# Top-k attention with a gated feed-forward: the left-over queries of each two batches moved next to each other, scores one slot sooner, another order of the first loads

## The chip, the cores and the metric

The kernel runs on one core of one Trainium2 chip. Time is the device time of one execution in microseconds (us). Before the change it is 1578.04 us, the median of 9 runs (1575.66 to 1578.78).

The engines are named as in the profile: PE (matrix multiply; PEld is its weight load), DVE (vector), ACT (scalar and activation), POOL (GpSimd), SP (issues the DMAs). Each takes its instructions strictly in the order of the program and waits for the others by semaphores.

## The reference

Queries, keys and values are (8 batches, 8 heads, 576 positions, 64 wide), float32. In each row of 576 scores only the 32 largest stay; a softmax of these weights the values. The result, 4608 rows of 512, goes through a feed-forward layer.

```python
scores = scale * np.matmul(q, k.transpose(0, 1, 3, 2))
kth = np.partition(scores, -top_k, axis=-1)[..., -top_k:-top_k + 1]
scores = np.where(scores >= kth, scores, -1000000000.0)
attn = np.exp(scores - np.max(scores, axis=-1, keepdims=True))
attn = attn / (np.sum(attn, axis=-1, keepdims=True) + 1e-09)
x = np.matmul(attn, v)                 # then heads side by side: (4608, 512)
h = x @ w_in                           # 512 x 2048
g = h * np.clip(h + 3.0, 0.0, 6.0) / 6.0
out = g @ w_out                        # 2048 x 512
```

The feed-forward weights arrive as float64 and are converted to float32 bit by bit in the kernel.

## The kernel before

**Tiles.** Two heads make a Pair, two Pairs a Duo. 576 queries are four tiles of 128 and a left-over of 64. A full Duo is one tile of 128 queries for four heads: four rows of 576 scores on each partition (two halves u = 0 and 1, each two rows). A left-over Duo (`self.rest`) holds the 64 left-over queries of four heads, two heads on the lower and two on the upper partitions: one row for each half. Each batch has 8 full and 2 left-over Duos, 80 in all. The list `duos` sets their order.

**Slots.** A Duo is 8 slots. In each slot DVE does one of the four rounds of `top` for one half: MAX8 (L256) finds the 8 largest, MATCH_REPLACE8 (L260) takes them out. All other work is written into slots by hand. For Duo m, at slot 8m plus a number from the table `usual` or `behind`: the shift on POOL (L269, L272), the two exponentials on ACT (L279, L284) and the sum den (L289), its reciprocal on DVE (L293), the scaling on POOL (L303) and the split of the float32 words into 16 bit halves (L312), a DMA transpose issued by SP (flip, L318), the join of the halves (L324, on ACT for u = 0 and on POOL for u = 1, result eT), the weighted values on PE (pv, L344), and their copy into xT or xr on ACT (`place`, L354). The first half's exponentials stand at slot 4, its reciprocal at 9; the second half's at 8 and 13; values at 22, or 25 in most of the run; place one slot later. The last two Duos use a shorter table, `soon`.

`duos[m + 1].scores()` stands in slot 1 of Duo m: matmuls into the PSUM tile big (L222 and L225 for a left-over Duo, L232 and L238 for a full one), then copies into sc by ACT (L227, L228, or L239, L242). In a slot, scores come before the parts of that slot.

**Feed-forward.** When the second half of the heads of a query tile is placed, `queue` adds a block for its 128 rows: 8 pieces of 16 matmuls h (L371) and 8 pieces of 2 matmuls acc (L391). After every second h piece ACT makes g and hs (L379, L381), and POOL gates them two pieces later (L385, L386). The left-over queries of an even batch and of the odd one behind it share the 128 columns of xr, so their block is queued when the odd batch's left-over is placed. Each slot emits about one piece, half a piece in a left-over Duo, one eighth more where 24 or more pieces are left.

**Loads.** In the second half of a batch the Pairs of the next one are loaded by SP, turned by PE (L177) and copied by ACT (L179 to L183). The values of a batch replace those of the batch before (L163, L167); their loads stand in slot 3 of its second and third Duo. Landed data, transposed queries and keys, e16, t16, eT and the raw weights st share the 14 buffers of one pool.

**Weights.** In the first four Duos each slot also moves the conversion of a weight chunk on (32 chunks): ACT makes a and y (L108, L111), POOL bounds a (L109), DVE shifts and merges (L117, L118), POOL adds (L123). a and y live in the 8 buffers of the pool that also holds g.

The order of left-over Duos before: in batches 0 to 2 both behind the last full tile, in 3 to 6 one behind tile 0 and one behind tile 2, in 7 both behind tile 0.

Of the kernel before, what the change touches and what calls it, by code (L numbers as in the profile page):

```python
# [29 lines left out]
def kernel(  # L30
# [9 lines left out]
    nc = tc.nc  # L40
# [47 lines left out]
    def big():  # L88

        return ps_big.tile([P, 5 * 512], F32, tag="big", name="big")  # L90
# [5 lines left out]
    def convert(dst, src):  # L96

        st = kqpool.tile([P, 2 * WC], U32, tag="kq", name="st")
        nc.sync.dma_start(st[:], src)
        yield
        words = st[:].rearrange("p (n two) -> p n two", two=2)
        lo, hi = words[:, :, 0], words[:, :, 1]
        a = gpool.tile([P, WC], F32, tag="g", name="a")
        y = gpool.tile([P, WC], F32, tag="g", name="y")
        nc.scalar.activation(a[:], hi.bitcast(F32), AF.Abs)  # L108
        nc.gpsimd.tensor_scalar(a[:], a[:], HI_MOST, HI_LEAST, ALU.min, ALU.max)  # L109

        nc.scalar.activation(y[:], lo, AF.Copy, bias=2.0, scale=2.0**-51)  # L111
        yield

        au, yu = a[:].bitcast(U32), y[:].bitcast(U32)
        nc.vector.tensor_scalar(au, au, 3, None, ALU.logical_shift_left)  # L117
        nc.vector.scalar_tensor_tensor(  # L118
            out=yu, in0=hi, scalar=0x80000000, in1=yu,
            op0=ALU.bitwise_and, op1=ALU.bitwise_or,  # L120
        )
        yield
        nc.gpsimd.tensor_tensor(  # L123
            dst.bitcast(I32), a[:].bitcast(I32), y[:].bitcast(I32), ALU.add
        )

    def weight_chunks():
# [11 lines left out]
    class Pair:  # L139
# [3 lines left out]
            self.b, self.hp = b, hp  # L143
            self.vm, self.vr, self.kr = vms[hp], vrs[hp], krs[b % 2 * NHP + hp]

        def load(self):
            h0 = 2 * self.hp
            t = self.landed = kqpool.tile([P, 2 * J + 1, 2, D], F32, tag="kq", name="landed")
            for i, src in enumerate((k, q)):
                for hh in range(2):  # L150
                    nc.sync.dma_start(  # L151
                        t[:, i * J : (i + 1) * J, hh, :],
                        src[self.b, h0 + hh, 0:JP, :].rearrange("(p j) d -> p j d", j=J),
                    )
                nc.sync.dma_start(
                    t[i * R : (i + 1) * R, 2 * J, :, :],
                    src[self.b, h0 : h0 + 2, JP:S, :].rearrange("h s d -> s h d"),
                )
# [9 lines left out]
                    self.vr[hh * R : (hh + 1) * R, hh, :], v[self.b, h0 + hh, JP:S, :]  # L168
                )

        def transpose(self):
            kq = kqpool.tile([P, JP + S], F32, tag="kq", name="kq")
            self.kT, self.qT = kq[:, 0:JP], kq[:, JP : JP + S]
            ps = big()
            for j in range(2 * J + 1):
                rows = self.landed[:, j, :, :].rearrange("p h d -> p (h d)")
                nc.tensor.transpose(ps[:, j * P : (j + 1) * P], rows, ident[:])  # L177
            c0 = 2 * JP
            nc.scalar.copy(kq[:, 0:c0], ps[:, 0:c0])  # L179
            nc.scalar.copy(kq[:, c0 : c0 + R], ps[:, c0 + R : c0 + 2 * R])  # L180
            for hh in range(2):
                d = slice(hh * D, (hh + 1) * D)
                nc.scalar.copy(self.kr[d, hh, :], ps[d, c0 : c0 + R])  # L183

    class Duo:

# [14 lines left out]
        def scores(self, us=(0, 1)):  # L201

            if us[0] == 0:
                self.sc = scpool.tile([P, 2, 2 * (S + R)], F32, tag="sc", name="sc")
                self.den = mpool.tile([P, 2, 2], F32, tag="den", name="den")
            sc, nu = self.sc[:, us[0] : us[-1] + 1, :], len(us)
            ps = big()
            heads = [slice(0, D), slice(D, P)]
            qs = slice(self.qt * P, min(self.qt * P + P, S))
            banks = ps[:, 0 : 4 * 512].rearrange("p (n s) -> p n s", s=512)  # L210
            left = ps[:, 4 * 512 :]
            if self.rest:


                quarters = [
                    (i, hh, d, heads[u ^ hh])
                    for i, u in enumerate(us)
                    for hh, d in enumerate(heads)
                ]
                for i, hh, d, to in quarters:  # L220
                    pr = self.pairs[us[i]]
                    nc.tensor.matmul(banks[to, i, :], pr.qT[d, qs], pr.kT[d, :])  # L222
                for i, hh, d, to in quarters:
                    pr = self.pairs[us[i]]
                    nc.tensor.matmul(banks[to, 2 + i, 0:R], pr.qT[d, qs], pr.kr[d, hh, :])  # L225
                nc.gpsimd.memset(sc[:, :, S : S + R], 0.0)
                nc.scalar.copy(sc[:, :, 0:JP], banks[:, 0:nu, :])  # L227
                nc.scalar.copy(sc[:, :, JP:S], banks[:, 2 : 2 + nu, 0:R])  # L228
                return
            for i, u in enumerate(us):  # L230
                pr = self.pairs[u]
                nc.tensor.matmul(  # L232
                    left[:, i * P : (i + 1) * P], pr.qT[:, qs], pr.kr[:].rearrange("p h r -> p (h r)")
                )
            for i, u in enumerate(us):
                pr = self.pairs[u]
                for hh, d in enumerate(heads):
                    nc.tensor.matmul(banks[:, 2 * i + hh, :], pr.qT[d, qs], pr.kT[d, :])  # L238
            nc.scalar.copy(  # L239
                sc.rearrange("p u (h s) -> p (u h) s", h=2)[:, :, 0:JP], banks[:, 0 : 2 * nu, :]  # L240
            )
            nc.scalar.copy(  # L242
                sc[:, :, JP : JP + P], left[:, 0 : nu * P].rearrange("p (u r) -> p u r", r=P)
            )

        def row(self, u, t):
            return self.sc[:, u, t * S : (t + 1) * S]
# [162 lines left out]
    duos = []  # L410
    for b in range(B):
        halves = [pairs[b][0:2], pairs[b][2:4]]
        for qt in range(J):
            duos += [Duo(h, qt) for h in halves]


            if qt == (0 if b == B - 1 else J - 1) and not 2 < b < B - 1:
                duos += [Duo(h, J) for h in halves]
            elif 2 < b < B - 1 and qt % 2 == 0:
                duos.append(Duo(halves[qt // 2], J))  # L420
    assert J == NHP == 4
    per_batch = 2 * J + 2
    ND = len(duos)
# [68 lines left out]
    def land(count=1):  # L492

        for _ in range(min(count, len(chunks))):
            c = convert(*chunks.pop(0))
            next(c)
            landing.append(c)

    def convert_step():


        for c in adding:
            next(c, None)
        adding.clear()
        if len(converting) >= 2 or not landing:
            for c in converting[:1]:
                next(c)
            adding.extend(converting[:1])
            del converting[:1]
        if landing:  # L510
            c = landing.pop(0)
            next(c)
            converting.append(c)
        land()
# [4 lines left out]
        return pairs[b + 1][at - first] if b + 1 < B and 0 <= at - first < NHP else None  # L519

    first = pairs[0]
    first[0].load()
    land(2)
    first[1].load()
    first[0].transpose()
    convert_step()
    duos[0].scores((0,))
    convert_step()
    first[2].load()
    convert_step()  # L530
    first[1].transpose()
    duos[0].scores((1,))
    land()

# [5 lines left out]
        shift1=7, exp1=8, inverse1=13, weights1=14, flip1=16, join1=19, values=22, place=23,  # L540
    )

    behind = dict(usual, values=25, place=26)
    early = dict(
        shift0=3, exp0=3, inverse0=4, weights0=4, flip0=5, join0=8,
        shift1=7, exp1=7, inverse1=8, weights1=8, flip1=9, join1=12, values=12, place=13,
# [29 lines left out]
    for m in range(ND + 3):  # L576
        u = duos[m] if m < ND else None
        for i in range(8):
            if u:
                u.top(i // 4, i % 4)  # L580
            if m < 4:
                parts(8 * m + i, False)
            convert_step()
            if m == 0 and i == 0:
                first[3].load()
            if m == 0 and i in (1, 2):
                first[i + 1].transpose()
            if i == (4 if m == 0 else 1) and m + 1 < ND:
                duos[m + 1].scores()
            if m < 4:  # L590
                parts(8 * m + i, True)
            else:
                parts(8 * m + i)
            if m == 0 and i in (1, 4):
                for p in duos[i // 4].pairs:
                    p.load_values()
            if i == 0:
                p = pair_at(m, 4)
                if p:
                    p.load()  # L600
            if i == 3 and u and u.pairs[0].b and 1 <= m % per_batch <= 2:
                for p in duos[m - 1].pairs:
                    p.load_values()
            if i == 5:
                p = pair_at(m, 5)
                if p:
                    p.transpose()

            due += ((left > 0) + (left >= 24) / 8 + (left >= 48) / 8) / (2 if u and u.rest else 1)
            piece(int(due))  # L610
            due -= int(due)
# [36 lines left out]
```

## Time and profile before

| what | value |
|---|---|
| median of 9 runs | 1578.04 us |
| profiled execution, its own time | 1578.04 us |
| its span, first to last instruction | 1576.3 us |
| DVE busy | 1466.7 us (93%) |
| PE busy, PEld busy | 1444.8 us (92%), 1033.7 us (66%) |
| POOL, ACT busy | 1143.1 us (73%), 1097.3 us (70%) |
| mean granted PE clock | 0.961 of full speed |
| DVE MAX8 (L256), all forms | 1152 of about 0.75 us |
| DVE MATCH_REPLACE8 (L260) | 864 of about 0.74 us |

Busy time is the time in which an engine has an instruction under way; matmuls overlap in their pipeline, so a busy PE need not be at its peak. The trace counts a float32 matmul as two instructions, the built order as one. In a timeline line the first number is the start and the second the time taken, both in us, with neighbouring instructions of one kind merged and their number behind an x.

### The profile page before, as it was taken

The numbers are of one execution on the slowest core, as the hardware profiler recorded it, in microseconds if no ns is written. First come the engines' busy times: TensorE is split into PE (matmuls) and PEld (weight loads), VectorE is DVE, ScalarE is ACT, GpSimd is POOL, SyncE is SP. The second block draws the span as 40 slices with busy tenths as digits, with TensorE's granted clock in tenths as the row PEclk, the third lists the DMA queues.
The fourth block names the chain that finished last, engine by engine and source line by source line (L and its number), as shares of the span: only waits on it lengthen the run. The fifth ranks groups of instructions, "written<-read, shape, count | busy, mean of one in ns | idle before, by whom it ended". The sixth has DMA issues, their size and how long they took to land.

```text
span 1576.3 us, 28787 instructions
## 1 busy us (share of the span) xinstructions
PE 1444.8 (92%) x10272; PEld 1033.7 (66%) x10272; DVE 1466.7 (93%) x3105; ACT 1097.3 (70%) x1865; POOL 1143.1 (73%) x1264
## 2 busy tenths in 40 slices
PE   5356799879999999998999999998999999999899
PEld 3142666567767767776777777766777777776675
DVE  6999999999999999999999999999999999999700
ACT  6675776777877777777776786777776786777521
POOL 4868687777867777867687777867687777867831
PEclk9577899989999999999999999999999999999999
DMA  8552544444444543545254544445254443533410
GB/s 237 156 185 42 116 83 79 92 94 99 73 94 86 101 85 78 98 88 116 54 105 81 98 88 83 94 91 113 58 104 81 98 88 82 103 58 68 83 22 14
DMA packets 450319, 144.49 MB, mean 92 GB/s; under 512 B 433280, under 2 KB 441472, under 8 KB 450176
## 3 DMA queue, kind: packets, MB, share of 16 engines
q1 hardware_dynamic: 450176, 142.65, 43.9%
q8 instruction: 81, 1.33, 0.3%
q14 instruction: 62, 0.51, 0.1%
HBM read 45.09 MB, written 9.44 MB: 35 GB/s over the span
## 4 chain that ended last, share of the span: by engine, by line
DVE 75%; PE 14%; issue 4%; POOL 3%; ACT 2%; SPq 1%; DMA 0%; POOLq 0%
DVE m L256 39%; DVE wk L260 34%; PE acc L391 6%; PE h L371 6%; PE pv L344 2%; DVE y L118 1%; DVE a L117 1%; PE big L238 1%; POOL eT L324 1%; POOL e L312 1%; DVE den L293 1%; POOL sc L303 1%; SPq L151 1%; POOL g L386 0%; ACT sc L284 0%
## 5 line engine op out<-in xcount | busy, mean ns | idle before, releaser
L256 DVE MAX8 m<-wk 128x8 f32<-128x576 f32 x864 | 614.3, 749 | 2.2
L391 PE MATMUL acc<-w_out,g 128*128 128x512 f32 x1152 | 519.8, 602 | 16.4 <-POOL g L386 16.4
L371 PE MATMUL h<-xT,w_in 128*128 128x128 f32 x4096 | 484.4, 279 | 18.4 <-ACT xT L354 18.4
L371 PEld LDWEIGHTS h<-xT,w_in 128*128 128x128 f32 x4096 | 473.9, 195 | 40.6 <-ACT xT L354 18.4
L260 DVE MATCH_REPLACE8 wk<-m,wk 128x576 f32<-128x576 f32 x576 | 424.5, 745 | 0.0
L303 POOL TENSOR_SCALAR sc<-sc,den 128x576 f32<-128x576 f32 x288 | 213.2, 750 | 241.0 <-DVE den L293 222.2
L391 PEld LDWEIGHTS acc<-w_out,g 128*128 128x128 f32 x1152 | 214.1, 192 | 264.9 <-issue 239.7
L312 POOL COPY e<-sc 128x2304 uint16<-128x2304 uint16 (+1 forms) x192 | 320.0, 1677 | 10.1
L279 ACT ACTIVATE sc<-sc,m 128x576 f32<-128x576 f32 x288 | 209.8, 774 | 74.1 <-DVE m L256 73.8
L284 ACT ACTIVATE sc<-sc,shift 128x576 f32<-128x576 f32 x288 | 220.2, 768 | 51.8 <-POOL shift L272 49.7
L324 ACT COPY eT<-t 128x2304 uint16<-128x2304 uint16 (+1 forms) x82 | 215.9, 2633 | 45.2 <-DMA t<-e 40.4
L344 PE MATMUL pv<-eT,vm 128*64 128x128 f32 (+1 forms) x2560 | 163.9, 273 | 57.5 <-ACT eT L324 44.1
L260 DVE MATCH_REPLACE8 wk<-m,sc 128x576 f32<-128x576 f32 x288 | 212.2, 744 | 0.0
L324 POOL COPY eT<-t 128x2304 uint16<-128x2304 uint16 (+1 forms) x78 | 203.6, 2611 | 4.5 <-DMA t<-e 4.3
L344 PEld LDWEIGHTS pv<-eT,vm 128*64 128x64 f32 x2560 | 135.0, 141 | 108.7 <-ACT eT L324 49.0
L256 DVE MAX8 m<-sc 128x8 f32<-128x576 f32 x288 | 203.7, 745 | 1.7 <-ACT sc L242 1.7
L386 POOL TENSOR_TENSOR g<-g,hs 128x512 f32<-128x512 f32 x144 | 184.7, 1283 | 12.1
L379 ACT ACTIVATE g<-h,three 128x512 f32<-128x512 f32 x144 | 98.4, 683 | 135.4 <-PE h L371 124.7
L238 PE MATMUL big<-kq 64*128 64x512 f32 x512 | 136.0, 651 | 0.0
L239 ACT COPY sc<-big 128x2048 f32<-128x2048 f32 (+1 forms) x65 | 119.2, 1833 | 18.1 <-PE big L238 17.9
L385 POOL TENSOR_SCALAR g<-g 128x512 f32<-128x512 f32 x144 | 89.0, 618 | 51.9 <-ACT g L379 40.7
L381 ACT COPY hs<-h 128x512 f32<-128x512 f32 x144 | 83.4, 579 | 0.0
(47 smaller groups left out, 1027.7 us busy)
## 6 DMA issues: line engine op xcount, KB each, us to landing
landed<-in_k_dram SPq DMA_DIRECT2D x64, 128.0 KB, 3.1
landed<-in_q_dram SPq DMA_DIRECT2D x64, 128.0 KB, 3.0
st<-in_moe_w_in_dram SPq DMA_DIRECT2D x16, 512.0 KB, 5.2
vm<-in_v_dram SPq DMA_DIRECT2D x64, 128.0 KB, 2.4
st<-in_moe_w_out_dram SPq DMA_DIRECT2D x16, 512.0 KB, 6.3
out_dram<-o SPq DMA_DIRECT2D x32, 256.0 KB, 2.4
t<-e SPq DMA_TRANSPOSE x160, 4.6
landed<-in_k_dram SPq DMA_DIRECT2D x32, 32.0 KB, 2.7
```

What stands on the lines that cost most here:

```text
L238: nc.tensor.matmul(banks[:, 2 * i + hh, :], pr.qT[d, qs], pr.kT[d, :])
L256: nc.vector.max(self.m[u][:, t, 8 * r : 8 * r + 8], self.cur[t])
L260: nc.vector.match_replace(wk, self.m[u][:, t, 8 * r : 8 * r + 8], self.cur[t], LOWEST)
L279: nc.scalar.activation(row, row, AF.Prelu, bias=m[:, t, TOP_K - 1 : TOP_K], scale=-1.0, alpha=FLAT)
L284: nc.scalar.activation(row, row, AF.Exp, bias=self.less[u][:, t : t + 1], scale=-scale / FLAT, accum_out=self.den[:, u, t : t + 1],)
L303: nc.gpsimd.tensor_scalar(row, row, self.den[:, u, t : t + 1], 1.0, ALU.mult, ALU.mult)
L312: nc.gpsimd.tensor_copy(halves[:, :, to : to + c1 - c0], words)
L324: copy(eT[:, 0 : self.nb, :] .rearrange("p c q -> p (c q)") .bitcast(U16) .rearrange("p (x h) -> p h x", h=2), self.t16[u][:, 0 : 2 * self ...
L344: nc.tensor.matmul(pv[hh * D : (hh + 1) * D, u * w : (u + 1) * w], pr.vm[:, hh, c, :] if c < J else pr.vr[:, hh, :], rhs, start=(c == 0), ...
L371: nc.tensor.matmul(h[:, (f - f0) * P : (f - f0 + 1) * P], w_in[:, i, f * P : (f + 1) * P], xT[:, i, :], start=(i == 0), stop=(i == NHP - 1),)
L386: nc.gpsimd.tensor_tensor(g[:], g[:], hs[:], ALU.mult)
L391: nc.tensor.matmul(acc[:], gs[f // nf][:, f % nf * P : (f % nf + 1) * P], w_out[:, f, :], start=(f == 0), stop=(f == NFC - 1),)
```

## The change

1. **Order of the Duos.** The left-over Duos of an even batch come last in it, those of an odd batch first: four left-over Duos stand in a row at the border of batches 0 and 1, 2 and 3, 4 and 5, 6 and 7.
2. **Scores** of the next Duo stand in slot 0 instead of 1 (Duo 0 keeps its own place), so before the second exponentials of the Duo before, which stand in slot 0 too. In the table `behind` values move from 25 to 24, place from 26 to 25.
3. **The first batch.** The q of the first Pair is loaded from ACT's queue, while k is loaded from SP's; one weight chunk is loaded behind each of the second and third Pair instead of two behind the first; the fourth Pair is loaded before the loop instead of in its first slot. The first Pair is turned through three small PSUM tiles with smaller copies, of which two wait until the first scores are copied. The first half's scores are copied in three pieces, the left-over columns first. Ahead of it all DVE fills a slice of w_out with zeros and PE does two matmuls on it.
4. **Conversion.** y has no buffer of its own any more; it is made in place in the converted weights.

```diff
-        y = gpool.tile([P, WC], F32, tag="g", name="y")
...
-        nc.scalar.activation(y[:], lo, AF.Copy, bias=2.0, scale=2.0**-51)
+        nc.scalar.activation(dst, lo, AF.Copy, bias=2.0, scale=2.0**-51)
...
-        def load(self):
+        def load(self, queue=None):
...
-            for i, src in enumerate((k, q)):
+            for i, (src, eng) in enumerate(((k, nc.sync), (q, queue or nc.sync))):
...
+            if first:
+                ps = [ps_w.tile([P, 512], F32, tag="w", name="kqp") for _ in range(3)]
+                turn(ps[0], range(J))
+                turn(ps[1], [J, 2 * J])
+                turn(ps[2], range(J + 1, 2 * J))
+                nc.scalar.copy(self.kT, ps[0][:])
+                nc.scalar.copy(kq[:, JP : JP + P], ps[1][:, 0:P])
+                copy_left(ps[1][:, P:])
+                self.later = [
+                    (kq[:, JP + P : c0], ps[2][:, 0 : JP - P]),
+                    (kq[:, c0 : c0 + R], ps[1][:, P + R : 2 * P]),
+                ]
+                return
...
+            if us == (0,):
+                (to, src), rest = copies
+                copies = [rest, (to[:, 0, :], src[:, 0, :]), (to[:, 1, :], src[:, 1, :])]
...
-        for qt in range(J):
+        for qt in [J, *range(J)] if b % 2 else range(J + 1):
             duos += [Duo(h, qt) for h in halves]
-            if qt == (0 if b == B - 1 else J - 1) and not 2 < b < B - 1:
-                duos += [Duo(h, J) for h in halves]
-            elif 2 < b < B - 1 and qt % 2 == 0:
-                duos.append(Duo(halves[qt // 2], J))
...
-    first[0].load()
-    land(2)
+    nc.vector.memset(w_out[:, 0, :], 0.0)
+    ps = big()
+    for _ in range(2):
+        nc.tensor.matmul(ps[:, 0:DM], w_out[:, 0, 0:P], w_out[:, 0, :])
+    first[0].load(nc.scalar)
     first[1].load()
-    first[0].transpose()
+    land()
+    first[2].load()
+    land()
+    first[0].transpose(first=True)
+    duos[0].scores((0,))
+    for copy in first[0].later:
+        nc.scalar.copy(*copy)
     convert_step()
-    duos[0].scores((0,))
+    first[3].load()
+    first[1].transpose()
     convert_step()
-    first[2].load()
-    convert_step()
-    first[1].transpose()
     duos[0].scores((1,))
...
-    behind = dict(usual, values=25, place=26)
+    behind = dict(usual, values=24, place=25)
...
-            if m == 0 and i == 0:
-                first[3].load()
...
-            if i == (4 if m == 0 else 1) and m + 1 < ND:
+            if i == (4 if m == 0 else 0) and m + 1 < ND:
                 duos[m + 1].scores()
```

More of the change, by code (lines that the diff above doesn't have):

```diff
@@ L106, in convert @@
         a = gpool.tile([P, WC], F32, tag="g", name="a")
-        y = gpool.tile([P, WC], F32, tag="g", name="y")
         nc.scalar.activation(a[:], hi.bitcast(F32), AF.Abs)
         nc.gpsimd.tensor_scalar(a[:], a[:], HI_MOST, HI_LEAST, ALU.min, ALU.max)
-        nc.scalar.activation(y[:], lo, AF.Copy, bias=2.0, scale=2.0**-51)
+        nc.scalar.activation(dst, lo, AF.Copy, bias=2.0, scale=2.0**-51)
         yield
-        au, yu = a[:].bitcast(U32), y[:].bitcast(U32)
+        au = a[:].bitcast(U32)
         nc.vector.tensor_scalar(au, au, 3, None, ALU.logical_shift_left)
         nc.vector.scalar_tensor_tensor(
-            out=yu, in0=hi, scalar=0x80000000, in1=yu,
+            out=dst.bitcast(U32), in0=hi, scalar=0x80000000, in1=dst.bitcast(U32),
             op0=ALU.bitwise_and, op1=ALU.bitwise_or,
@@ L123, in convert @@
         nc.gpsimd.tensor_tensor(
-            dst.bitcast(I32), a[:].bitcast(I32), y[:].bitcast(I32), ALU.add
+            dst.bitcast(I32), a[:].bitcast(I32), dst.bitcast(I32), ALU.add
         )
@@ L144, in __init__ @@
             self.vm, self.vr, self.kr = vms[hp], vrs[hp], krs[b % 2 * NHP + hp]
-        def load(self):
+        def load(self, queue=None):
             h0 = 2 * self.hp
             t = self.landed = kqpool.tile([P, 2 * J + 1, 2, D], F32, tag="kq", name="landed")
-            for i, src in enumerate((k, q)):
+            for i, (src, eng) in enumerate(((k, nc.sync), (q, queue or nc.sync))):
                 for hh in range(2):
-                    nc.sync.dma_start(
+                    eng.dma_start(
                         t[:, i * J : (i + 1) * J, hh, :],
@@ L154, in load @@
                     )
-                nc.sync.dma_start(
+                eng.dma_start(
                     t[i * R : (i + 1) * R, 2 * J, :, :],
@@ L169, in load_values, with transpose, turn, copy_left @@
                 )
-        def transpose(self):
+        def transpose(self, first=False):
             kq = kqpool.tile([P, JP + S], F32, tag="kq", name="kq")
             self.kT, self.qT = kq[:, 0:JP], kq[:, JP : JP + S]
+            c0 = 2 * JP
+            def turn(ps, tiles):
+                for i, j in enumerate(tiles):
+                    rows = self.landed[:, j, :, :].rearrange("p h d -> p (h d)")
+                    nc.tensor.transpose(ps[:, i * P : (i + 1) * P], rows, ident[:])
+            def copy_left(ps):
+                for hh in range(2):
+                    d = slice(hh * D, (hh + 1) * D)
+                    nc.scalar.copy(self.kr[d, hh, :], ps[d, 0:R])
+            if first:
[11 more added lines that the diff above has]
+                return
             ps = big()
[L175 to L178, printed above, removed]
+            turn(ps, range(2 * J + 1))
             nc.scalar.copy(kq[:, 0:c0], ps[:, 0:c0])
             nc.scalar.copy(kq[:, c0 : c0 + R], ps[:, c0 + R : c0 + 2 * R])
-            for hh in range(2):
-                d = slice(hh * D, (hh + 1) * D)
-                nc.scalar.copy(self.kr[d, hh, :], ps[d, c0 : c0 + R])
+            copy_left(ps[:, c0:])
     class Duo:
@@ L238, in scores @@
                     nc.tensor.matmul(banks[:, 2 * i + hh, :], pr.qT[d, qs], pr.kT[d, :])
[L239 to L244, printed above, removed]
+            copies = [
+                (sc.rearrange("p u (h s) -> p (u h) s", h=2)[:, :, 0:JP], banks[:, 0 : 2 * nu, :]),
+                (sc[:, :, JP : JP + P], left[:, 0 : nu * P].rearrange("p (u r) -> p u r", r=P)),
+            ]
+            if us == (0,):
+                (to, src), rest = copies
+                copies = [rest, (to[:, 0, :], src[:, 0, :]), (to[:, 1, :], src[:, 1, :])]
+            for copy in copies:
+                nc.scalar.copy(*copy)
         def row(self, u, t):
@@ L521 @@
     first = pairs[0]
-    first[0].load()
-    land(2)
-    first[1].load()
-    first[0].transpose()
+    nc.vector.memset(w_out[:, 0, :], 0.0)
[3 more added lines that the diff above has]
+    first[0].load(nc.scalar)
+    first[1].load()
+    land()
[4 more added lines that the diff above has]
+    for copy in first[0].later:
+        nc.scalar.copy(*copy)
     convert_step()
-    duos[0].scores((0,))
+    first[3].load()
+    first[1].transpose()
     convert_step()
-    first[2].load()
-    convert_step()
-    first[1].transpose()
     duos[0].scores((1,))
```

## The prediction

> **What bounds the kernel now.** I read, in this order: the waits of VectorE (DVE), busy time by stretch, the chain that ended last, the waits of the stretch 300 to 335 us, and the timeline around two left-over duos. A "duo" is one step of the top-k loop; I number them 0 to 79 and call T28 the start of duo 28 on DVE.
>
> DVE's waits, whole span (us, times, longest):
>
> ```profile
> DVE a L117 <- POOL a L109: 13.3, 2, 10.0
> DVE den L293 <- ACT den L289: 7.3, 2, 6.7
> DVE m L256 <- ACT sc L242: 1.7, 1, 1.7
> ```
>
> The 10.0 and the 1.7 lie before the first MAX8 at 13.59; the 6.7 lies behind the last one, which ends at 1488.5. Between the two DVE idles 3.3 + 0.6 = 3.9 us. Two stretches, top-k and what follows it (span, then PE, PEld, DVE, ACT, POOL busy):
>
> ```profile
> 13.59:1488.50 1474.91, 1360.10 (x9813) 975.62 (x9813) 1465.44 (x3101) 1072.80 (x1824) 1108.39 (x1215) 0.96 0.46 95
> 1488.50:1576.30 87.80, 79.53 (x444) 55.43 (x444) 0.19 (x2) 19.30 (x33) 31.63 (x31) 0.96 0.10 23
> ```
>
> So: 13.6 us of start, 1475 us in which DVE is full, 87.8 us of tail in which TensorE (PE) alone works. The chain from 1490 on says at what:
>
> ```profile
> 1490.20 2.69 POOL eT L324
> ...
> 1492.93 2.40 PE pv L344 x20
> 1495.34 4.80 PE h L371 x32
> 1500.14 10.30 PE acc L391 x24
> 1510.44 2.33 PE pv L344 x40
> 1512.77 3.63 PE acc L391 x8
> 1516.40 14.29 PE h L371 x128
> 1530.69 13.73 PE acc L391 x32
> 1544.43 14.29 PE h L371 x128
> 1558.72 13.75 PE acc L391 x32
> ```
>
> From 1495 PE does feed-forward work without a hole, 59.7 us of it behind the last weighted values (pv): a backlog. And PE once had nothing to do, with the whole top-k running:
>
> ```profile
> PE h L371 <- ACT xT L354: 9.3, 1, 9.3
> PE big L232 <- ACT sc L242: 3.8, 1, 3.8
> PE pv L344 <- POOL eT L324: 1.7, 1, 1.7
> ```
>
> These three waits (300 to 335 us) make 14.8 us, after which the granted clock is lower too (0.77 over 300 to 330).
>
> **Part 1, the order of the duos: the tail.** One block of 16 pieces costs 14.29 + 13.73 = 28.0 us, 1.75 us a piece. I counted the feed-forward matmuls in the built order of both programs. Behind the last pv the old order has 2 pieces and two blocks (34), the new one 1 h piece, 8 acc pieces and one block (25): 9 x 1.75 = 15.8 us less. Between the last two pv stand 8 pieces in both: 4.80 + 10.30 = 15.1 us before, now 1 acc (1.7) and 7 h (12.5) = 14.2: 0.9 less. Two smaller terms: on POOL a gate (0.61 + 1.26 us, at 1488.24) stood ahead of the join that ended at 1492.89, and no longer does: 1.9 sooner. But the acc pair now stands between that pv and the next h, whose xT ACT places behind the scaling of that acc (0.60 + 0.37): 1.1 later. Tail: -15.8 - 0.9 - 0.8 = **-17.5 us**. It counts only if the 9 pieces really run earlier under DVE. The counts at equal duos: before scores 20 the old order has 98 pieces done, the new one 103; at 28, 159 and 167; at 79, 519 and 527. At 13 the new one is behind (49 to 58): it keeps pieces for the stretch in which PE idled 14.8 us, because the left-over block of batches 0 and 1 is ready a batch's length earlier.
>
> **Can PE carry it?** A full duo takes DVE 19.41 us (T21 to T22). On PE it costs 8 x 1.75 + scores 2.56 (589.47 to 592.03) + pv 2.34 = 18.9. A left-over duo takes DVE 11.27 us, and PE 4 x 1.75 + scores 1.13 + pv 2.34 = 10.5. With 8 transposes of 1.2 us a pair of batches is 16 x 18.9 + 4 x 10.5 + 9.6 = 354 of DVE's 356 us. It fits, with little to spare. At the end PE may be 5 us late for nothing: it waited 2.4 + 4.4 us for joins between 1479 and 1493.
>
> **Part 2, four left-over duos in a row, scores one slot sooner: DVE.** The bound is the reciprocal (L293) of a left-over duo's second half. Around duos 28 and 29, ACT, POOL and DVE:
>
> ```profile
> 595.62 0.22 POOL L272 TENSOR_SCALAR shift<-shift 128x1 f32<-128x1 f32 x1
> 596.77 0.20 ACT L289 ACTIVATE den<-den 128x1 f32<-128x1 f32 x1
> 597.37 0.15 DVE L293 RECIPROCAL den<-den 128x1 f32<-128x1 f32 x1
> ```
>
> DVE came 0.4 us after den was ready; in the other clusters (duos 8, 18, 72) 2.4, 1.8 and 2.2 us. POOL is what is late: the shift of a half whose tops ended at 588.4 came at 595.6, behind a join (2.76), two scalings and a split (1.47 + 2.10), two gates. Moving scores ahead puts ACT's copies (0.99 + 0.27 for a left-over duo, 1.86 + 0.38 for a full one) before the exponentials of the half before (prelu, exp, den); here ACT was idle 3.0 us for that shift, so the first copy fits in the hole. The gates fall better in the new piece count: in duos 28 to 31 none, 2, 2, none, where the old order had three in duo 28's time. POOL in duo 29: scalings and splits 2 x (0.75 + 1.59), join 2.8, shifts 0.85, memset 0.2, gates 3.9 = 12.4 of 11.27 us; in duo 30, with the shorter join of 1.9, 11.5; in duo 31, 7.6. So about 1.4 us is added to a lag that was tolerated, then it is worked off. Ends: nothing, as in the four pairs of before; or 0.9 us for each of the second and third duo and 1.8 for the fourth, with 4 clusters 14 us. I take 2: **+2 us**, nearest to the rows of the pairs. What is queued behind ACT's copy if PE's scores come late: that exponential, the reciprocal on DVE, hence all. The loads of v now start in the fourth left-over duo and wait on SP for pv of the first; 8 issues of about 0.55 us (624.2 to 629.7) delay one flip by some 2 us, and so one join on ACT; the next duo is a full one whose reciprocal stands 14.6 us after its start: covered, 2 us a cluster if not.
>
> **Part 3, the start.** The first q load goes from behind k on SP (issue 2.82 to 4.77, landed 6.64) to ACT's queue at about 0.7: landed with k at some 5 us. The 9 transposes (2.2 us) then end near 7.2 instead of 7.97, and the first scores need a 512 column copy (about 0.6) and a short one instead of 1.01 + 0.22; their own copy is cut, so the first row is ready after 0.27 + 0.6. I get kr at 7.7, scores to 10.5, first MAX8 at 11.3 instead of 13.59: 2.3 us. But DVE did one conversion (0.43 + 0.68) before that MAX8, and it now stands behind: net -1.2. The extra memset and two matmuls run before any load lands. Bounds: the 2.3 us in full, and +1 if the earlier first[3] load makes the conversions wait (DMA is full from 5 to 30 us). **-1.2 us.**
>
> DMA: Bandwidth & Descriptors of the Trainium skill ("Issuing engines are not separate DMA queues") says a second issuing engine saves only the sequencer's time, since all share the 16 DMA engines. By it the move is worth at most the 2.1 us of issue that q stood behind, and k and q still share the bytes; the first-MAX8 gain would be about 1.5 instead of 2.3, and the sum 0.8 us higher.
>
> For the two matmuls on zeros the row is: 9 transposes took 2.18 us at 13.61 and 1.20 at 583.73. The page TensorE: Matmul & The Clock Gate of the Trainium skill ("Part 1: The HAM clock gate") has the clock released after some 3.4 us of sustained work; by it two matmuls followed by a wait for a load would not do, and if they did, the sum would be some 2 us lower. I count nothing.
>
> **Part 4, one buffer less per conversion.** ACT waited 9.06 us at 134.8 for a g buffer that a conversion held (L123), and behind it came the DVE stall of 3.29 at 137.3. Without y half as many buffers are held. Ends 0 and -3.3: **-2.5 us**. The conversions' work is unchanged.
>
> **Sum:** -17.5 + 2 - 1.2 - 2.5 = -19.2. The profiled execution took 1578.04 us (span 1576.3 and 1.74 around it), equal to the median 1578.04. 1578.04 - 19.2 = 1558.8, say **1559 us**.
>
> **Rivals.** (a) Clusters stall DVE at L293: for it the 0.4 us slack, against it the free ACT hole and POOL's count. At the upper end 14 us instead of 2: 1571. (b) PE becomes the bound: 354 of 356 leaves no room for holes like those of 4.7 and 4.3 us at 718 and 1083. If each of three pairs of batches loses 4 us beyond its room, scores come late and DVE waits for sc: 3 x 2.4 = 7, 1566. Against it: those holes are waits for ACT behind DVE's own tops, when PE was ahead. (c) Slower: ACT's queue locks. In each left-over duo ACT sits in the scores copy until PE delivers, the exponential waits behind it, and DVE waits at L293. Without the +2 the gains are 21.2 us; 16 left-over duos, so it decides from 21.2 / 16 = 1.3 us each; at 2.5 us each 40 - 21.2, 1597. For it: PE reached pv 2 to 4 us after the start of such duos. Against: it now does the scores one piece sooner. (d) The change does not shorten the tail: PE is 16 us late at duo 78 and the 9 pieces run after DVE's end all the same. 1559 + 17.5 = 1576, no change. Against it: PE's 7 us of waits just before the end.
>
> **How the numbers follow.** Forecast 0.67, its own range 1552 to 1566; (a) 0.12, (b) 0.10, (c) 0.06, (d) 0.05. The range 1551 to 1572 takes in (a) and (b) and leaves out (c) and (d). 0.2% is 3.2 us, about what a measurement of this kernel tells from none. Faster: the first three, and a little of (d): 0.90; same 0.04; slower 0.06.
>
> **What would show it.** Tail: from DVE's last MAX8 to the end about 70 us, 43.6 of PE work behind the last pv. PE without the hole near 317. DVE: first MAX8 near 11.3, no wait near 137, den waits between 200 and 1480 summing to about 2 us. Wrong would be DVE waits at L293 or for sc of over 1 us in each left-over duo, or a PE that no longer waits for joins before the last two pv.

## The result: 1587.46 us, slower by 9.2 us

The changed kernel takes 1587.46 us (median of 9 runs, 1586.28 to 1588.32) against 1578.27 us (29 runs of the kernel before). The ratio is 1.0059, 95% interval 1.0051 to 1.0068. The prediction was 1559 us: wrong in sign, 28 us off. The profiled execution took 1587.46 us (span 1585.7).

The three sections into which the prediction cut the span, from both traces:

| section | before | after | difference | predicted |
|---|---|---|---|---|
| start, up to the first MAX8 | 13.59 | 9.96 | -3.6 | -2.3 |
| first MAX8 to the end of the last | 1474.91 | 1506.05 | +31.1 | +0.6 |
| tail behind the last MAX8 | 87.80 | 69.69 | -18.1 | -17.5 |

(Predicted for the middle: 2 for the clusters, 1.1 for the conversion that moves in, less 2.5.) Tail and start are as predicted or better; the start owes its better part to a faster PE in this execution (last section). The middle lost more than both gained.

The lines of the changed kernel have other numbers than those of the kernel before: scores are copied at L249 and L250 (left-over duo) or L269 (full duo), behind the matmuls L244 and L247 or L260; the exponentials are L304 and L309, den L314, its reciprocal L318; xT and xr are placed at L379, the h pieces are L396, the acc pieces L416. Busy time by stretch of the changed kernel (start and end, length, then PE, PEld, DVE, ACT, POOL, granted clock, DMA share, GB/s):

```profile
9.96:1516.01 1506.05, 1369.28 (x9848) 980.19 (x9849) 1470.95 (x3103) 1076.77 (x1833) 1113.76 (x1224) 0.96 0.46 94
1516.01:1585.70 69.69, 65.86 (x410) 46.73 (x408) 0.17 (x1) 16.96 (x29) 24.03 (x23) 0.99 0.12 29
```

DVE's work in the middle grew by only 5.5 us (1465.44 to 1470.95). The rest is idle time, and DVE's waits name its end (us in total, times, longest):

```profile
DVE den L318 <- ACT den L314: 33.0, 18, 4.7
DVE m L281 <- ACT sc L269: 8.5, 1, 8.5
DVE a L116 <- POOL a L108: 1.3, 2, 0.9
```

Before, the wait of the reciprocal for den was 7.3 us, twice, and one of the two (6.7) lay behind the last MAX8. Now 4.7 of the 33.0 lie there. Inside the middle DVE waits 33.0 - 4.7 + 1.3 = 29.6 us instead of 3.9: +25.7 of the +31.1. The weight conversions on DVE account for another 3.4 (58.5 instead of 55.1 us) and the conversion that moved behind the first MAX8 for 1.1; 0.9 I did not assign.

One place shows the mechanism: duo 28, the first of a row of four left-over duos, in which the reciprocal of duo 27's second half is due. DVE, ACT and PE of the changed kernel there (start, us taken; in brackets the idle time before it and its releaser):

```profile
589.58 0.76 DVE L281 MAX8 m<-wk 128x8 f32<-128x576 f32 x1
...
595.89 0.17 DVE L318 RECIPROCAL den<-den 128x2 f32<-128x2 f32 x1 [4.70 <-ACT den L314]
```
```profile
586.67 2.80 ACT L349 COPY eT<-t 128x2304 uint16<-128x2304 uint16 x1
591.60 1.01 ACT L249 COPY sc<-big 128x1024 f32<-128x1024 f32 x1 [2.13 <-PE big L247]
592.51 0.27 ACT L250 COPY sc<-big 128x128 f32<-128x128 f32 x1
592.66 1.45 ACT L304 ACTIVATE sc<-sc,m 128x576 f32<-128x576 f32 x2
...
595.65 0.20 ACT L314 ACTIVATE den<-den 128x2 f32<-128x2 f32 x1
```
```profile
585.00 5.32 PE L416 MATMUL acc<-w_out,g 128*128 128x512 f32 x12
590.25 1.09 PE L244 MATMUL big<-kq 64*64 64x512 f32 x8
591.16 0.29 PE L247 MATMUL big<-kr,kq 64*64 64x64 f32 x8
```

POOL's shift for the half was done at 588.00 (it starts at 587.79 and takes 0.21). ACT was free from 589.5. But the next thing in its queue is the copy of duo 29's scores, and PE, busy with acc pieces up to 590.25, delivers these only at 591.45. So ACT sits idle 2.13 us, copies (1.06 us to the start of the next), and only then does the exponentials for which DVE waits 4.70 us. Waits of 4.7 us stand in the same place in the two later rows of four, near 953 and 1315. The page PSUM — Partial Sum Buffer of the Trainium skill ("Engine vs sequencer instructions") says that ACT's queue is strict FIFO; this row agrees, since exponentials with all inputs ready stood 3.2 us behind the start of ACT's wait (589.47 to 592.66).

The waits of the whole stretch 170 to 1480 us in the changed kernel:

```profile
ACT sc L269 <- PE big L260: 119.9, 50, 5.8
PE h L396 <- ACT xT L379: 27.7, 20, 1.4
DVE den L318 <- ACT den L314: 22.4, 14, 4.7
```

ACT now waits 120 us for PE's scores where in the kernel before it was 13.4. PE in turn waits for xT, 20 times 1.4 us, at the start of a block, because ACT places xT behind those exponentials and behind the scaling of the block before. Of two things predicted to go, DVE's wait of 3.29 at 137 has vanished, and the wait of PE near 317 (9.3 on ACT's xT) has only become shorter: 4.9 at 309, on xr. The tail, in the chain that ended last:

```profile
1521.37 1.91 PE acc L416 x4
1523.28 12.51 PE h L396 x112
1535.79 2.33 PE pv L369 x40
1538.12 1.98 PE h L396 x16
1540.10 13.73 PE acc L416 x32
1553.84 14.29 PE h L396 x128
1568.13 13.75 PE acc L416 x32
```

An h piece is 8 matmuls, 16 instructions of the trace; an acc piece is 2 matmuls, 4 instructions. Between the last two pv stand 1 acc and 7 h pieces, behind the last one 1.98 + 13.73 + 14.29 + 13.75 = 43.8 us of PE work. The prediction has the same pieces and 43.6.

### The profile page after: what moved, and what is told of

Its sections match the earlier page's. It is cut to its first block, busy times and chain, and to the rows that moved or that the text cites. A ratio compares the mean times of both kernels' runs of the same rounds, so it can differ in the third digit from the quotient of the medians.

```text
span 1585.7 us, 28762 instructions
## 1 busy us (share of the span) xinstructions
PE 1441.6 (91%) x10276; PEld 1029.7 (65%) x10276; DVE 1471.7 (93%) x3106; ACT 1096.9 (69%) x1868; POOL 1140.2 (72%) x1264
## 3 DMA queue, kind: packets, MB, share of 16 engines
q1 hardware_dynamic: 448976, 142.36, 43.8%
## 4 chain that ended last, share of the span: by engine, by line
PE 58%; DVE 24%; ACT 9%; POOL 4%; issue 3%; SPq 1%; DMA 1%; ACTq 0%; POOLq 0%
PE h L396 24%; PE acc L416 21%; DVE m L281 12%; DVE wk L285 9%; PE big L260 5%; PE pv L369 5%; ACT sc L269 3%; ACT sc L309 3%; PE big L180 1%; DVE a L116 1%; ACT sc L304 1%; PE big L254 1%; DVE w_out L117 1%; POOL e L337 1%; POOL eT L349 1%
## 5 line engine op out<-in xcount | busy, mean ns | idle before, releaser
L416 PE MATMUL acc<-w_out,g 128*128 128x512 f32 x1152 | 520.6, 602 | 11.6 <-POOL g L411 11.6
L396 PE MATMUL h<-xT,w_in 128*128 128x128 f32 x4096 | 483.3, 277 | 30.1 <-ACT xT L379 30.1
L396 PEld LDWEIGHTS h<-xT,w_in 128*128 128x128 f32 x4096 | 469.5, 192 | 57.2 <-ACT xT L379 33.8
L416 PEld LDWEIGHTS acc<-w_out,g 128*128 128x128 f32 x1152 | 213.9, 192 | 255.5 <-issue 235.6
L337 POOL COPY e<-sc 128x2304 uint16<-128x2304 uint16 (+1 forms) x192 | 320.1, 1677 | 10.1
L309 ACT ACTIVATE sc<-sc,shift 128x576 f32<-128x576 f32 x288 | 220.4, 769 | 35.0 <-POOL shift L297 32.2
L304 ACT ACTIVATE sc<-sc,m 128x576 f32<-128x576 f32 x288 | 210.8, 781 | 31.5 <-DVE m L281 31.3
L269 ACT COPY sc<-big 128x256 f32<-128x256 f32 (+3 forms) x131 | 137.1, 1100 | 131.7 <-PE big L260 121.6
L260 PE MATMUL big<-kq 64*128 64x512 f32 x512 | 132.6, 637 | 0.0
```

Of the source, the lines that this page charges most:

```text
L269: nc.scalar.copy(*copy)
L304: nc.scalar.activation(row, row, AF.Prelu, bias=m[:, t, TOP_K - 1 : TOP_K], scale=-1.0, alpha=FLAT)
L309: nc.scalar.activation(row, row, AF.Exp, bias=self.less[u][:, t : t + 1], scale=-scale / FLAT, accum_out=self.den[:, u, t : t + 1],)
L337: nc.gpsimd.tensor_copy(halves[:, :, to : to + c1 - c0], words)
L396: nc.tensor.matmul(h[:, (f - f0) * P : (f - f0 + 1) * P], w_in[:, i, f * P : (f + 1) * P], xT[:, i, :], start=(i == 0), stop=(i == NHP - 1),)
L416: nc.tensor.matmul(acc[:], gs[f // nf][:, f % nf * P : (f % nf + 1) * P], w_out[:, f, :], start=(f == 0), stop=(f == NFC - 1),)
```

## The experiments

Theory A: the place of the scores in ACT's queue (ahead of the second half's exponentials) turns PE's lateness into waits of DVE. Rivals: B, four left-over duos in a row cost this by themselves; C, PE is made late by the holes in front of each block, which come from the scaling of o standing ahead of xT on ACT; D, start and conversion. All ratios are against the kernel before, measured on the same chip.

**Scores back to slot 1** (values and place one slot later again), the rest of the change kept:

```diff
-    behind = dict(usual, values=24, place=25)
+    behind = dict(usual, values=25, place=26)
-            if i == (4 if m == 0 else 0) and m + 1 < ND:
+            if i == (4 if m == 0 else 1) and m + 1 < ND:
```

> The changed kernel with the scores back in slot 1 and values, place back at 25, 26; order of the duos, start and conversion stay changed. In the changed kernel PE's scores are late, ACT copies them (2.14 us) and only then does the second exponentials (3.1 us) and, behind these, the scaling of acc and the place of xT. Theory A (that order on ACT costs: it delays den, so DVE waits 26 us more, and it opens a hole of 1.43 us on PE at each block, which keeps PE late): with the exponentials ahead again both go; about 1560 us, DVE waits for den between 200 and 1480 us under 5 us. Theory B (four left-over duos in a row overload POOL, ACT and PE by themselves): the den waits at the borders of the batches stay, about 1583 us. Theory C (PE is full whatever the order): about 1578 us, DVE waits for scores instead of den.

Measured: 1569.31 us, ratio 0.9944 (0.9928 to 0.9961). The middle is 1484.2 us instead of 1506.1, the tail 71.6. This small edit is worth 18.2 us. Waits of the stretch 170 to 1480:

```profile
ACT sc L269 <- PE big L260: 37.3, 17, 4.0
PE h L396 <- ACT xT L379: 10.6, 21, 0.5
DVE den L318 <- ACT den L314: 5.3, 2, 3.7
```

B is out as the main cause: the rows of four are unchanged here. But the edit moves two things, ACT's order and PE's.

**Exponentials first.** Scores stay in slot 0 and values in 24. From duo 4 on, what the second half has due in that slot (its exponentials, and where it falls there its shift) comes ahead of the next duo's scores.

```diff
-            if i == (4 if m == 0 else 0) and m + 1 < ND:
+            if i == (4 if m == 0 else 0) and m + 1 < ND and m < 4:
                 duos[m + 1].scores()
...
             else:
+                if i == 0 and m + 1 < ND:
+                    exps = [x for x in queued.get(8 * m, []) if x[1] in ("shift1", "exp1")]
+                    for n, part in exps:
+                        getattr(duos[n], part[:-1])(1)
+                        queued[8 * m].remove((n, part))
+                    duos[m + 1].scores()
                 parts(8 * m + i)
```

> The changed kernel with only one thing undone: from duo 4 on, shift and exponentials of the second half stand ahead of the scores in slot 0 again; scores stay in slot 0, values at 24. Theory A: about 1560 us, as with the slots back, den waits gone, no PE hole of 1.43 us at the blocks. Theory B: about 1585 us, den waits of 4 to 5 us at each border of batches stay. Theory C: den waits are replaced by waits for scores, about 1580 us.

Measured: 1565.20 us, 0.9919 (0.9904 to 0.9934), 22.3 us below the changed kernel and 13 us below the kernel before: the best version of all. The middle is 1483.6 us. ACT at the same place, which comes 4 us earlier:

```profile
584.26 0.77 ACT L309 ACTIVATE sc<-sc,shift 128x576 f32<-128x576 f32 x1
...
585.91 0.20 ACT L314 ACTIVATE den<-den 128x2 f32<-128x2 f32 x1
586.14 1.01 ACT L249 COPY sc<-big 128x1024 f32<-128x1024 f32 x1
587.04 0.27 ACT L250 COPY sc<-big 128x128 f32<-128x128 f32 x1
```

The copy now comes behind den, without an idle time before it: PE finished the scores while ACT did the exponentials. ACT's wait for PE's scores falls from 119.9 to 14.0 us, DVE's waits in the middle from 29.6 to 7.9. PE, DVE and POOL have the same instructions in the same order in both kernels; ACT has the same ones in another order. Theory A is shown: the order of two groups in ACT's queue is worth 22 us here.

**The old order of duos, the rest of the change kept:**

```diff
-        for qt in [J, *range(J)] if b % 2 else range(J + 1):
+        for qt in range(J):
             duos += [Duo(h, qt) for h in halves]
+            if qt == (0 if b == B - 1 else J - 1) and not 2 < b < B - 1:
+                duos += [Duo(h, J) for h in halves]
+            elif 2 < b < B - 1 and qt % 2 == 0:
+                duos.append(Duo(halves[qt // 2], J))
```

> The changed kernel with the old order of the duos; scores in slot 0, values at 24, start and conversion stay changed. Theory A: the scores' place hurts here too, though less, since PE has a backlog of blocks and does not wait for the place of xT: the tail is 88 us again, DVE waits for den; 1578 to 1588 us. Theory B: without four in a row the den waits go, the start's gain is left: about 1574 us. Theory C: about 1574 us.

Measured: 1583.52 us, 1.0038 (1.0023 to 1.0053). The tail is 85.7 us again and DVE's waits in the middle are 9.1 us instead of 29.6. So the early scores do far less harm in the old order, and the first experiment has the new order without the harm: it takes both.

**The scaling of o later.** The store of a finished block, with the scaling in front of it, is emitted two pieces later, so that ACT places xT first:

```diff
-                if f == NFC - 1:
-                    o = opool.tile([P, DM], F32, tag="o", name="o")
-                    nc.scalar.mul(o[:], acc[:], 1.0 / 6.0)
-                    for p0, p1, dst in rows:
-                        nc.sync.dma_start(dst, o[p0:p1, :])
-                yield None
+                if f < NFC - 1:
+                    yield None
+        def finish():
+            o = opool.tile([P, DM], F32, tag="o", name="o")
+            nc.scalar.mul(o[:], acc[:], 1.0 / 6.0)
+            for p0, p1, dst in rows:
+                nc.sync.dma_start(dst, o[p0:p1, :])
+        yield finish
```

> The changed kernel with the scaling of acc and its store issued two pieces later, so that the place of xT stands ahead of it on ACT. Theory A: the hole of 1.43 us on PE at each block shrinks by the 0.58 us of the scaling to about 0.85; PE is late by less, den waits fall from 26 to about 12 us: about 1574 us. Theory B: the waits at the borders stay, about 1583 us. Theory C: PE gains 36 times 0.58 = 21 us less what it cannot use: about 1568 us.

Measured: 1585.64 us, 1.0049 (1.0034 to 1.0064), only 1.8 us below the changed kernel. Theory A said about 1574 and theory C about 1568; the time lies nearest to the 1583 of theory B, which the two experiments with the same rows of four, at 1569.31 and 1565.20 us, speak against. Waits of the stretch 170 to 1480:

```profile
DVE den L318 <- ACT den L314: 21.1, 15, 3.2
ACT sc L269 <- PE big L260: 102.2, 41, 6.1
PE h L396 <- ACT xT L379: 18.1, 19, 1.1
```

The holes did shrink (27.7 to 18.1 us), and PE fell back less: the weighted values of duo 24 start 65.2 us behind that duo's start, against 69.8 in the changed kernel and 65.8 in the one with exponentials first. With the good version's lag at that duo, DVE still waits 28.5 us in the middle; the waits are smaller and more. The holes went rather more than half of the way to the 10.9 us that they have with exponentials first, and hardly any time came back. So the holes, theory C, do not set the time by themselves; what stands behind the late scores in ACT's queue does.

**Each part alone, on the kernel before.** The new order alone, the early slots alone (scores in slot 0, values 24, place 25), the new start with the conversion without y alone:

> The kernel before with the new order of the duos alone. Theory A (the scores' place ahead of the exponentials is what costs): the tail is 17 to 18 us shorter, DVE waits at the borders of batches stay under 6 us: about 1568 us. Theory B (the four left-over duos in a row cost by themselves): about 1580 us. The step of the prediction on the tail stands if the last MAX8 ends about 70 us before the span does.

> The kernel before with scores in slot 0, values at 24 and place at 25, nothing else. Theory A: DVE waits for den in several left-over duos and the tail stays at 88 us; 1581 to 1585 us. Theory B: 1576 to 1578 us.

> The kernel before with the new start and the conversion without y, old order and old slots. In the changed kernel MAX8 starts 3.9 us earlier, but duo 4 starts 0.7 us later than before. If the start is worth nothing: 1578 us, duo 4 at about 144 us. As predicted (start -1.2, conversion -2.5): 1574 us.

| new start | order | scores | us | ratio (95%) | middle | tail |
|---|---|---|---|---|---|---|
| no | new | slot 1 | 1569.14 | 0.9942 (0.9927 to 0.9957) | 1483.6 | 71.4 |
| no | old | slot 0 | 1584.02 | 1.0037 (1.0024 to 1.0051) | 1481.5 | 87.2 |
| yes | old | slot 1 | 1578.78 | 1.0006 (0.9997 to 1.0014) | 1480.0 | 88.4 |
| yes | new | slot 1 (first experiment) | 1569.31 | 0.9944 (0.9928 to 0.9961) | 1484.2 | 71.6 |
| yes | old | slot 0 (third experiment) | 1583.52 | 1.0038 (1.0023 to 1.0053) | 1484.9 | 85.7 |
| yes | new | slot 0 (the change) | 1587.46 | 1.0059 (1.0051 to 1.0068) | 1506.1 | 69.7 |

By medians against the kernel before on the same chip (1577.92), the three parts alone give -8.8 + 6.1 + 0.9 = -1.8 us; together they give +9.2. The last four rows, with the new start throughout, show the interaction: early scores cost 4.7 us with the old order and 18.2 with the new one.

Where it comes from shows at duo 28, a left-over duo in either order. The copy of its scores, in the kernel with the early slots alone and in the changed one:

```profile
558.88 1.01 ACT L227 COPY sc<-big 128x1024 f32<-128x1024 f32 x1 [2.03 <-PE big L225]
```
```profile
573.86 1.02 ACT L249 COPY sc<-big 128x1024 f32<-128x1024 f32 x1
574.76 0.29 ACT L250 COPY sc<-big 128x128 f32<-128x128 f32 x1
```

Duo 27 started on DVE at 558.25 in the first kernel and at 561.96 in the second: the copy starts 0.6 us behind that with the old order, 11.9 with the new one. In the new order 16 full duos run in a row (12 to 27), without a left-over duo in which PE can catch up; in the old one 8 did here. The lateness harms nobody as long as only scores wait for it, since DVE needs them a whole duo later. The order alone still costs DVE 8.5 us more waits than before in the middle (12.4 in all; the longest for den there, 5.0, lies in the row at duo 28):

```profile
DVE den L293 <- ACT den L289: 15.0, 5, 5.9
DVE a L117 <- POOL a L109: 13.4, 2, 10.1
```

(The 5.9 lies behind the last MAX8, the 10.1 before the first.) The tail gains about twice that, -16.4.

The start alone is worth nothing that can be measured. Its first MAX8 came 3.5 us earlier (10.14) and the stall at 137 was gone, yet duo 4 started on DVE at 146.0 instead of 144.4. The groups of DVE's conversions up to 150 us, before and then with the new start alone (busy us, mean ns of one, idle time before):

```profile
L118 DVE SCALAR_TENSOR_TENSOR y<-st,y 128x512 uint32<-128x512 uint32 x32 | 30.0, 938 | 0.0
L117 DVE TENSOR_SCALAR a<-a 128x512 uint32<-128x512 uint32 x32 | 25.1, 783 | 13.3 <-POOL a L109 13.3
```
```profile
L116 DVE TENSOR_SCALAR a<-a 128x512 uint32<-128x512 uint32 x32 | 25.9, 810 | 1.9 <-POOL a L108 1.8
L117 DVE SCALAR_TENSOR_TENSOR w_out<-st,w_out 128x512 uint32<-128x512 uint32 x16 | 17.4, 1088 | 0.0
L117 DVE SCALAR_TENSOR_TENSOR w_in<-st,w_in 128x512 uint32<-128x512 uint32 x16 | 15.3, 958 | 0.0
```

With the merge made straight into the weights, the merges take DVE 17.4 + 15.3 - 30.0 = 2.7 us more and the shifts beside them 0.8. Together with the conversion that moved behind the first MAX8 (1.1), a new wait of 1.8 for POOL's a and a den wait of 2.3 at the second half of duo 0 (0.6 before), that eats the gain.

**Exponentials first, with y back.** The conversion gets its own buffer y again, on top of the best version:

```diff
+        y = gpool.tile([P, WC], F32, tag="g", name="y")
-        nc.scalar.activation(dst, lo, AF.Copy, bias=2.0, scale=2.0**-51)
+        nc.scalar.activation(y[:], lo, AF.Copy, bias=2.0, scale=2.0**-51)
```

(and y in place of the destination in the two merges behind it)

> The version with the exponentials ahead of the scores, with a buffer of its own for y again. If the missing y is why the conversions take 3.4 us more on DVE: L116 and L117 sum to about 55 us again, and the time falls from 1565 by up to 3 us, less what the wait for a g buffer brings back (3.3 us before). If y does not matter: 1565 us.

Measured: 1570.22 us, 0.9951 (0.9939 to 0.9964), 5.0 us slower than without y. DVE's waits between 100 and 160 us:

```profile
DVE a L117 <- POOL a L109: 6.9, 2, 3.6
```

The conversions are 3.6 us shorter with y, but two stalls for g buffers come back, 6.9 us, and in all DVE waits 17.5 us in the middle instead of 7.9. So the lost buffer is worth 5 us in this version, in the way that part 4 of the prediction said; in the kernel before, which has one such stall of 3.3, it pays for the slower merges and no more.

Whether early scores harm at all once PE is on time can be read within the traces. In the changed kernel the copy of the next scores starts 1.6 to 9.3 us behind a left-over duo's start on DVE. In the eight left-over duos in which that is 4.8 us or less, DVE does not wait at the reciprocal; in the eight in which it is 5.4 us or more, it does, from 0.6 us up to the three of 4.7, where the copy comes last of all. Duo 28 again, in the kernel with the early slots alone:

```profile
578.46 1.03 ACT L227 COPY sc<-big 128x1024 f32<-128x1024 f32 x1
```

The duo started at 577.66, the copy stands in the same place ahead of the exponentials, 0.8 us later, and DVE does not wait. In the changed kernel the duo starts at 582.34 and the copy at 591.60. So early scores cost where their copy comes late, which in duos 28, 48 and 68 is 2.13 us of waiting for PE on top of ACT's own backlog. Not measured: the changed kernel with less work on PE, which would show the same by an edit; and exponentials first with the old start.

## Why the prediction was wrong, point by point

- **Part 1, the tail: right.** -17.5 predicted, -18.1 measured, with the same pieces in the chain. Its proviso, that the 9 pieces run earlier under DVE, held too. Alone on the kernel before, the new order shortens the tail by 16.4 and gains 8.8 in all.
- **Part 2, the step that failed:** "here ACT was idle 3.0 us for that shift, so the first copy fits in the hole". It took the hole of the kernel before, with its order and PE's lead there, and filled it with an instruction that itself waits. At duo 28 POOL's shift, which the step held to be the late one, was done at 588.00; the copy waited for PE until 591.6. The term was +2 and measured about +26, of which about 8.5 are the rows of four (the order alone) and about 18 the early scores on top of them (the first experiment).
- **"Can PE carry it?"** Its sum, 354 of 356 us a pair of batches, was of totals. PE's work did fit: with the same PE instructions the best version's middle is 22 us shorter. But 18.9 us of PE in a full duo of 19.41 says nothing of when the scores inside it are ready. Over duos 12 to 24 the weighted values slip by 3.4 us in the best version and by 9.0 in the changed kernel (62.4 to 65.8 us and 60.8 to 69.8 behind the duo's start).
- **The rivals.** (c) was the mechanism: ACT sits in the scores copy, the exponentials wait, DVE waits at the reciprocal. It got 0.06. The condition was 1.3 us for each of 16 left-over duos, 21 us in all; measured were 22.4 us between 170 and 1480 in 14 waits, few of them large (three of 4.7), rather than an even 1.3. What was argued against it, "it now does the scores one piece sooner", compares with PE's queue and not with ACT's, where the scores moved past the exponentials. (a), the reciprocal stalls, named the place but its upper end of 14 us was half of what came. (b) and (d) fell: DVE never waited for scores in the middle, and the tail shortened.
- **Part 3, the start.** First MAX8 at 9.96 instead of the 11.3 predicted, but all of the gain was lost again before duo 4. That it came earlier than predicted is luck: with the same start, but with PE slow (scores back to slot 1, see the last section), the first MAX8 comes at 11.93. So loads and copies gave about 1.7 us, less than the 2.3 predicted; the rest was PE's speed, counted at nothing. The 1.7 is near the 1.5 that the prediction worked out as an estimate from DMA: Bandwidth & Descriptors of the Trainium skill ("Issuing engines are not separate DMA queues").
- **Part 4, "the conversions' work is unchanged"**: wrong by 3.4 us, which is more than the -2.5 put in for the stall.
- **The sum.** Tail, start and conversion were off by some 2 us together. The range failed by one term.

## What to carry to other kernels

An idle time on an engine is no room for an instruction that waits for another engine: in a queue that runs in order, ask what stands behind it, and put work whose inputs are ready ahead of it (22 us here for swapping two groups in ACT's queue). A balance of an engine's totals doesn't say when it delivers; follow one result from its producer to the queue that reads it, with the new order's lateness and not the old one's. What a part of a change costs can depend on the other parts (the early scores 4.7 us with the old order, 18.2 with the new one), so run the corners (order and slots) before judging either.

## What the runs showed of the hardware that was not expected

The two matmuls on zeros, counted at nothing, were followed by a faster PE in most of the kernels that have them, and not in all. PE before and after, first microseconds:

```profile
4.80 1.08 PE L177 MATMUL big<-ident,landed 128*128 128x128 f32 x4 [4.80 <-DMA landed<-in_k_dram]
6.67 1.30 PE L177 MATMUL big<-ident,landed 128*128 128x128 f32 x5 [0.78 <-DMA landed<-in_q_dram]
...
10.25 2.08 PE L238 MATMUL big<-kq 64*128 64x512 f32 x4
```
```profile
1.47 3.74 PE L548 MATMUL big<-w_out 128*128 128x512 f32 x4 [1.47 <-DVE w_out L545]
5.77 1.17 PE L180 MATMUL kqp<-ident,landed 128*128 128x128 f32 x9 [0.56 <-DMA landed<-in_k_dram]
...
8.00 1.13 PE L260 MATMUL big<-kq 64*128 64x512 f32 x4
```

Nine transposes take 1.17 us instead of 2.38, four score matmuls 1.13 instead of 2.08. The granted clock in the stretches reads 1.00 in both kernels, so only the durations show it. The matmuls on zeros lasted 3.74 us, and the next work came 0.56 us behind them. The same start in the kernel of the first experiment, with the scores back in slot 1:

```profile
1.47 3.78 PE L548 MATMUL big<-w_out 128*128 128x512 f32 x4 [1.47 <-DVE w_out L545]
6.03 2.15 PE L180 MATMUL kqp<-ident,landed 128*128 128x128 f32 x9 [0.78 <-DMA landed<-in_k_dram]
...
9.02 2.08 PE L260 MATMUL big<-kq 64*128 64x512 f32 x4
```

Here nothing became faster behind the same matmuls, which lasted 3.78 us, and the first MAX8 came at 11.93. With exponentials first and with the old order, the transposes are still slow (1.95 and 1.76) and the scores fast (1.13), first MAX8 at 10.49 and 10.50; in the other three with this start both are fast. Each of these is one profiled execution. TensorE: Matmul & The Clock Gate of the Trainium skill ("Part 1: The HAM clock gate") asks for about 3.4 us of sustained work: six of the seven executions fit that, and in the first experiment 3.78 us did not do. The same section says that the point of release varies from run to run, and the seven executions agree. The prediction's reading of it, that two matmuls would not do, did not work out how long they last; it holds for one execution of the seven.

The merge of a conversion on DVE takes 0.94 us on average into y, 0.96 into w_in and 1.09 into w_out, with the same shapes. The destination need not be the reason: in the traces of before, the changed kernel, the new start alone and both versions with exponentials first, every merge that ran with nothing on POOL beside it took about 0.68 us, and every one of 1.09 us or more ran beside an instruction of POOL. There are 12 such long ones of 32 before, 15 in the changed kernel. No run here says why some merges beside POOL are long and others are not.
